# An attention block with its projections woven in: the fill between a slot's two logit products, and two engines in program order

## The chip, the cores and the metric

The kernel runs on one core of one Trainium2 chip. The metric is the device time of one execution in microseconds (us), lower is better; of several runs the median is taken. A profile shows one execution more closely.

The engines of the core run side by side, each through its own list of instructions, and meet by semaphores: TensorE (PE; its weight loads are listed as PEld), VectorE (DVE), ScalarE (ACT), GpSimd (POOL) and SyncE (SP), which here issues the transfers between HBM and the core's memory.

## The reference, cut to what matters

One transformer block over 2048 rows of 512, in float32: a layer norm modulated by a condition, "infini-attention" with 32 heads of 16 in four segments of 512 rows, a second modulated layer norm, and a bilinear feed-forward part of width 1376.

```python
mod = (silu(c) @ w_mod).reshape(1, 6, 1, -1)
sa, ca, ga, sb, cb, gb = mod[:, 0], ..., mod[:, 5]
h = layernorm(x) * (1 + ca) + sa
q, k, v = heads(h @ wq), heads(h @ wk), heads(h @ wv)       # 32 heads of 16, 4 segments of 512
phi = lambda t: where(t > 0, t + 1, exp(t))
for s in range(4):
    logits = q_s @ k_s.T * 0.25 + mask                      # within the segment, causal
    a_dot = softmax(logits) @ v_s
    a_mem = (phi(q_s) @ M) / (phi(q_s) @ z + 1e-6)
    out_s = g * a_mem + (1 - g) * a_dot                     # g = sigmoid(beta), per head
    M, z = M + phi(k_s).T @ v_s, z + phi(k_s).sum(rows)
x = x + ga * (out @ wo)
h = layernorm(x) * (1 + cb) + sb
return x + gb * (((h @ w_gate) * (h @ w_up)) @ w_down)
```

## The kernel before

**Order.** Every matmul and transposition goes through `pe`, which chains it to the one before: TensorE runs in the order in which the program text calls it, written out by hand. What VectorE, ScalarE, GpSimd and SP run is ordered by a scheduler, which plays the program through with its own costs and picks, on each engine, among the instructions that are ready. In the prologue alone (segment 0, group 0) VectorE and ScalarE are called through `CV` and `CA`, two objects of `class Chain`, which tie each instruction to the one before it on its engine, so that they too keep the program's order. `pin` ties single instructions to TensorE's place.

**The attention loop.** A unit is 4 heads of one segment, so there are 32 (`NQ`). The loop over `v` has five slots for each unit. A slot does one fifth of two different units:

- `q_step(u, i)`: logits with queries in rows, for the row maximum. The product goes to the PSUM bank `lq`, which exists once; two small matmuls add the mask, and VectorE reduces it (L261, tile `mxb`). The next `q` has to wait for that.
- `k_step(v, slot)`: logits again with keys in rows, with the negated maximum as two more rows of the operand. It goes to the bank `lk`, which exists once too; ScalarE takes the exponential (L295, tile `pt`), GpSimd sets the masked corner to zero (L298).
- `av_step` (slot 1): values times `pt` of the unit before, in bank `tb`, copied out by ScalarE as `tsb` (L324).
- `n_step` (slot 2): VectorE makes the negated maximum `nm` (L267), TensorE transposes it (`ntp`), VectorE writes it as two bfloat16 parts `nt` (L272, L273), and two transfers put it in rows 96 and 97 of `qst`, the operand of the next unit's `k`.
- `t_step` (slot 4): transposition of `tsb`, division by the sum (`rd`, `orow`, L345), and after every second unit a transfer to `od`.
- `fill(share[slot])`: the next pieces of what feeds later units and what follows done ones. Such a piece is mostly a block of three matmuls, ended by a `yield 0.68`. The shares are 0.25, 0, 0.25, 0.25, 0.25 of a rate. They run out of two generators: projections `kps`, `qps` (`a_kq`), values `vps` (`a_v`), layer norm (`ln`: `bn_stats` L139, normalisation L159, transposition `atp`/`ctp`, ScalarE's modulation L172), the memory part (`a_mem`: `mp`, `up`, `mz`), modulation rows (`mod`), and the output projection (`wo_op`: transposition `op` and copies `oH` L405, `oL` L408; `wo_mm`: `wops` and residual add L428).
- `load(v + 3)` at slot 1: transfers of `kst` and `qst` for a unit three further on.

**The end of a projection group.** When a group of `kps` or `qps` is complete, `a_kq` copies it out of PSUM as `f` (ScalarE, L632), splits it in three bfloat16 parts (high part on ScalarE L635, difference on GpSimd L636, middle part on ScalarE L637, rest on GpSimd L638), writes them out by three transfers to `kd` or `qd`, and, where the memory part needs phi, makes a relu and an exponential on ScalarE (L653, L654, called `rl` and `ph`) and joins them on VectorE (L658).

**The output weights.** `wo_prep` (woven in as `ob`) loads rows of `wo` (`wor`), scales them on GpSimd (L736), and splits them in `woH` (ScalarE, L748) and `woL` (GpSimd, L749), which `wops` needs.

After the loop stands the feed-forward part (`gps`, `ups`, `acc`).

Of the kernel before, what the change touches and what calls it, by code (L numbers as in the profile page):

```python
# [17 lines left out]
P = 128  # L18
# [27 lines left out]

@with_exitstack
def tile_kernel(ctx, tc, x, wq, wk_, wv, wo, beta, w_gate, w_up, w_down, c, w_mod, out):
# [31 lines left out]
    CV, CA = Chain(tc, nc.vector), Chain(tc, nc.scalar)  # L80
    cst = ctx.enter_context(tc.tile_pool(name="cst", bufs=1))
# [21 lines left out]
    nc.vector.memset(ones, 1.0)  # L103
    epst = cst.tile([P, 1], F32, name="epst")
    nc.vector.memset(epst, EPS)
    hmg = cst.tile([P, NG, HG, VS], F32, name="hmg")
    hm8 = cst.tile([P, HG], F32, name="hm8")
    nc.vector.tensor_reduce(hm8, ident.rearrange("p (d h) -> p h d", h=HG), axis=AX.X, op=ALU.add)
    for g in range(NG):
        nc.vector.tensor_copy(hmg[:, g], hm8.unsqueeze(2).to_broadcast([P, HG, VS]))  # L110
# [21 lines left out]
    def ln(pool, hpool, xt, s, sc, sh, pfx, hb, fast):  # L132

        first = pfx == "a" and s == 0
        V, A = (CV, CA) if first else (nc.vector, nc.scalar)
# [31 lines left out]
        for d in range(KT):  # L167
# [7 lines left out]
            if fast:  # L175
                V.tensor_copy(hi, h)
                V.tensor_sub(lo, h, hi.bitcast(F32))
            else:
                nc.scalar.activation(hi, h, AF.Copy)
                nc.gpsimd.tensor_sub(lo, h, hi.bitcast(F32))  # L180
# [30 lines left out]
    for a in mxb:  # L211
        nc.vector.memset(a, NEG)
    identb = ap.tile([P, P], BF, name="identb")
    nc.vector.tensor_copy(identb, ident)
    cmask = ap.tile([P, P], BF, name="cmask")
    nc.vector.memset(cmask, 0.0)
# [10 lines left out]
    def q_step(u, i):  # L227
# [33 lines left out]
        nc.vector.tensor_reduce(o, src, axis=AX.X, op=ALU.max)  # L261

    def n_step(u):
# [3 lines left out]
        nc.vector.tensor_reduce(nm, mxb[u % 2].rearrange("p h (q j) -> p (h q) j", j=4), axis=AX.X,  # L267
# [4 lines left out]
        nc.vector.tensor_copy(nt[:, 0], tp)  # L272
        nc.vector.tensor_sub(nt[:, 1], tp, nt[:, 0])  # L273
# [3 lines left out]
    def k_step(u, i):  # L277
# [17 lines left out]
        nc.scalar.activation(pt, kp, AF.Exp, scale=0.25)  # L295
# [6 lines left out]
    def av_step(u, kb):  # L302
# [19 lines left out]
        if kb == 2:  # L322
            tsbs[u] = ap.tile([P, L], F32, tag="tsb", name=f"tsb{u}", bufs=2)
            nc.scalar.activation(tsbs[u], tbs.pop(u), AF.Copy)  # L324

    def t_step(u):
# [15 lines left out]
        nc.vector.reciprocal(rd, tr[:, :, :, DH])  # L342
        og = omg[:, g * HG + h0:g * HG + h0 + 4]
        nc.vector.tensor_mul(rd, rd, og.unsqueeze(1).to_broadcast([P, 4, 4]))
        nc.vector.tensor_mul(orow[:, :, h0:h0 + 4, :], tr[:, :, :, 0:DH],  # L345
# [11 lines left out]
    def prep(i, pool, rpool, tag, nb):  # L357
# [9 lines left out]
        for nm in "gu":  # L367
# [3 lines left out]
            pin(nc.vector.tensor_copy(hi[:, :, 0:n], raw[:, :, 0:n]))  # L371
# [5 lines left out]
        pin(nc.vector.tensor_mul(rawd[0:n], rawd[0:n], gbb[0:n]))  # L377
        yield 0.0
        nc.scalar.activation(hi[0:n], rawd[0:n], AF.Copy)
# [14 lines left out]
    def wo_op(s, pb, rw, us, gs=range(NG)):  # L394

        for g in gs:
# [8 lines left out]
            nc.scalar.activation(oH, op, AF.Copy)  # L405
            us.append((oH, oL))
            yield 0.45
            pin(nc.vector.tensor_sub(oL, op, oH.bitcast(F32)))  # L408
# [18 lines left out]
    def wo_add(s, t, xr, ps):  # L427
        pin(nc.vector.tensor_add(xr, xr, ps))  # L428
        nc.sync.dma_start(x1d[s][t], xr)
# [42 lines left out]
    nc.vector.memset(wu, 0.0)  # L472
# [16 lines left out]
    nc.scalar.activation(e1, s_c, AF.Exp, scale=-1.0)  # L489
    nc.vector.tensor_scalar_add(e1, e1, 1.0)  # L490
    nc.vector.reciprocal(e1, e1)
    nc.vector.tensor_mul(s_c, s_c, e1)
    nc.scalar.activation(gg, be, AF.Exp, scale=-1.0)
    nc.scalar.activation(omg, be, AF.Exp)
    for tl in (gg, omg):
        nc.vector.tensor_scalar_add(tl, tl, 1.0)
        nc.vector.reciprocal(tl, tl)
# [4 lines left out]
    def mod_acc(r):  # L502
        for k in range(KT):
            pin(nc.scalar.activation(r[k], r[k], AF.Identity, scale=s_c[:, k:k + 1]))
# [4 lines left out]
    def cols(a, dst, nm):  # L509
# [3 lines left out]
        nc.vector.tensor_copy(dst, ps)  # L513

    def bcast(a, dst, nm):
        ps = bank(nm)
        MM(ps, ones, a, start=True, stop=True)
        nc.scalar.activation(dst, ps, AF.Copy)
# [48 lines left out]
    def load_g(nm, w, g):  # L567

        A, V = (CA, CV) if g == 0 else (nc.scalar, nc.gpsimd)
# [25 lines left out]
    def a_v(s):  # L595
        hH, hL = hcur[0]
        for t in range(4):
# [9 lines left out]
            nc.scalar.activation(vt[s % 2][t][:, 0:H * VS].rearrange("p (h e) -> p h e", e=VS)[:, :, 0:DH],  # L607
# [7 lines left out]
    def a_kq(s, g, nm):  # L615
# [3 lines left out]
        if True:  # L619
# [11 lines left out]
            A, V = (CA, CV) if fast else (nc.scalar, nc.gpsimd)  # L631
# [5 lines left out]
            (CV.tensor_copy if fast else nc.scalar.copy)(q3[:, 1, :], r)  # L637
            V.tensor_sub(q3[:, 2, :], r, q3[:, 1, :])  # L638
            for r0, n, k in ((0, 3, 0), (3, 2, 0), (5, 1, 0)) if nm == "k" else ((0, 1, 3), (3, 1, 2), (5, 1, 1)):
                if nm == "k":  # L640
                    nc.sync.dma_start(dst[s][g][r0:r0 + n].rearrange("r p t -> p r t"), q3[:, 0:n, :])
                else:
                    i = 3 - k
                    nc.sync.dma_start(dst[s][g][r0:r0 + k].rearrange("r p t -> p r t"),
                                      q3[:, i:i + 1, :].to_broadcast([P, k, L]))
            if (nm == "k" and s < NSEG - 1) or (nm == "q" and s > 0):
                if s == 0 and g == 0:
# [5 lines left out]
                nc.scalar.activation(rl, f, AF.Relu)  # L653
                nc.scalar.activation(e, f, AF.Exp)  # L654
# [23 lines left out]
    def a_mem(s, g):  # L678
# [3 lines left out]
        if s < NSEG - 1:  # L682
# [4 lines left out]
            nc.scalar.activation(pkr.rearrange("p a b -> p (a b)"), mp, AF.Copy)  # L687
            yield 0.5
        if s > 0:
# [3 lines left out]
            for i in range(2):  # L693
# [4 lines left out]
                nc.scalar.activation(ups[:, 2 * i:2 * i + 2], up, AF.Copy)  # L698
                yield 0.5
            pin(nc.vector.tensor_scalar_add(den, ups[:, :, :, DH], 1e-6))  # L700
            nc.vector.reciprocal(den, den)
            nc.gpsimd.tensor_mul(mem, ups[:, :, :, 0:DH], den.unsqueeze(3).to_broadcast([P, 4, HG, DH]))
            nc.sync.dma_start(memd[s][g], mem.rearrange("p t h e -> p (t h e)"))
        if s < NSEG - 1:
# [4 lines left out]
            if s == 0:  # L709
                nc.vector.tensor_mul(MZ[g], mz, hmg[:, g])  # L710
# [319 lines left out]
```

## Time and profile before

| | us |
|---|---|
| runs | 951.93, 954.98, 950.16 |
| median | 951.93 |
| profiled execution | 955.31 |
| its span (first to last instruction) | 953.6 |
| TensorE busy | 904.1 |
| VectorE, ScalarE, GpSimd busy | 461.8, 407.6, 315.6 |
| granted clock of TensorE, mean | 0.984 |

The profile's page gives the busy time of the engines, the chain of work that ended last, and the costliest groups, one in a line: line of the kernel, engine, operation, out<-in, shapes, count, then busy time and mean ns, then the idle time of the engine just ahead of these instructions and what released it. A timeline's row has start and duration in us, engine, line, operation, and in brackets the idle time ahead and its releaser. A row of the waits has the waiting operation, what it waited for, the total, the times and the longest. Rows of windows give start and end, length, busy time with the instruction count for PE, PEld, DVE, ACT and POOL, then the granted clock of TensorE (1.00 is full), the share of the DMA engines, and GB/s.

### The profile page before, as it was taken

What the parts mean: (1) busy time and instruction counts of PE and PEld (TensorE: products, weight loads), DVE (VectorE), ACT (ScalarE), POOL (GpSimd) and SP (SyncE); (2) the same over time, 40 slices, a digit from 0 to 9 for tenths busy, and PEclk for the clock granted to TensorE, in tenths of its full rate; (3) what the DMA queues carried; (4) which work ended last, traced back from release to release, by engine and by line L of the source; (5) the groups of instructions that cost most, each with busy time, mean ns of one, the idle gap of its engine ahead of it and who ended that gap; (6) DMA issues with size and microseconds to landing.
All of it is one profiled execution on the core that took longest, in us unless ns stands there. A gap on an engine that the chain in (4) does not pass through costs nothing.

```text
span 953.6 us, 14247 instructions
## 1 busy us (share of the span) xinstructions
PE 904.1 (95%) x5528; PEld 654.9 (69%) x5528; DVE 461.8 (48%) x756; ACT 407.6 (43%) x603; POOL 315.6 (33%) x457
## 2 busy tenths in 40 slices
PE   8979999999999999998998899999999999999998
PEld 5756657566566666665555577887888788878886
DVE  8566556675556755566457324544223223222112
ACT  3557757687575865577342621222111211221111
POOL 3255536465454753456522422562000000000000
PEclk9999999999999999999898899999999999999999
DMA  7574534654435544466661234432201020101011
GB/s 221 160 228 153 169 111 130 215 164 153 139 116 185 171 130 123 137 208 204 227 186 60 86 102 144 122 98 61 89 0 26 20 89 1 45 0 45 1 45 44
DMA packets 86211, 109.80 MB, mean 115 GB/s; under 512 B 9504, under 2 KB 58656, under 8 KB 86144
## 3 DMA queue, kind: packets, MB, share of 16 engines
q1 hardware_dynamic: 86000, 108.89, 36.8%
q8 instruction: 43, 0.70, 0.3%
q14 instruction: 24, 0.20, 0.1%
q10 hardware_dynamic: 144, 0.02, 0.0%
HBM read 67.98 MB, written 40.63 MB: 114 GB/s over the span
## 4 chain that ended last, share of the span: by engine, by line
PE 80%; DVE 7%; ACT 7%; DMA 3%; issue 1%; POOL 1%; SPq 0%; DVEq 0%; ACTq 0%; POOLq 0%
PE ups L966 13%; PE gps L966 13%; PE q L75 8%; PE tb L75 7%; PE k L75 6%; PE wops L75 5%; PE qps L75 4%; PE vps L75 3%; PE kps L75 3%; ACT pt L295 3%; DVE mxb L261 3%; PE acc2lq L987 2%; PE acc0lq L987 2%; PE acc3lq L987 2%; PE acc1lq L987 2%; PE acc1lk L987 2%
## 5 line engine op out<-in xcount | busy, mean ns | idle before, releaser
L261 DVE TENSOR_REDUCE mxb<-q 128x8 f32<-128x1024 f32 x160 | 195.5, 1222 | 161.2 <-PE q L75 160.8
L295 ACT ACTIVATE pt<-k 128x1024 f32<-128x1024 f32 x160 | 163.8, 1024 | 89.6 <-PE k L75 88.1
L298 POOL TENSOR_SCALAR_AFFINE_SELECT pt<-pt 128x256 f32<-128x256 f32 (+1 forms) x224 | 99.5, 458 | 202.5 <-ACT pt L295 194.5
L971 DVE TENSOR_TENSOR gs<-gs,ups 128x512 f32<-128x512 f32 (+1 forms) x44 | 30.2, 687 | 194.0 <-PE ups L966 194.0
L75 PE MATMUL q<-kst,qst 96*128 96x128 bf16 (+2 forms) x640 | 99.4, 278 | 14.8 <-DVE mxb L261 13.8
L75 PE MATMUL k<-qst,kst 98*128 98x384 bf16 (+3 forms) x512 | 98.1, 304 | 14.8 <-ACT pt L295 13.4
L970 ACT ACTIVATE gs<-gps 128x512 f32<-128x512 f32 (+1 forms) x44 | 26.2, 597 | 146.5 <-PE gps L966 146.5
L75 PEld LDWEIGHTS <-qst 96*128 96x128 bf16 x640 | 47.3, 99 | 54.4 <-issue 47.4
L974 ACT ACTIVATE mH<-gs 128x512 fp32r<-128x512 f32 (+1 forms) x44 | 27.8, 633 | 130.4 <-DVE gs L971 128.1
L75 PE MATMUL tb<-pt,v 128*32 128x512 f32 (+3 forms) x1024 | 76.6, 440 | 0.0
L966 PE MATMUL gps<-chH,gL 128*128 128x512 f32 (+1 forms) x176 | 69.3, 394 | 0.0
L966 PE MATMUL gps<-chH,gH 128*128 128x512 f32 (+1 forms) x176 | 69.3, 394 | 0.0
L966 PE MATMUL ups<-chH,uH 128*128 128x512 f32 (+1 forms) x176 | 69.3, 394 | 0.0
L966 PE MATMUL ups<-chL,uH 128*128 128x512 f32 (+1 forms) x176 | 69.3, 394 | 0.0
L966 PE MATMUL gps<-chL,gH 128*128 128x512 f32 (+1 forms) x176 | 69.3, 394 | 0.0
L966 PE MATMUL ups<-chH,uL 128*128 128x512 f32 (+1 forms) x176 | 69.2, 393 | 0.0
L75 PEld LDWEIGHTS <-kst 98*128 98x128 bf16 x512 | 41.5, 98 | 38.4 <-issue 31.7
L75 PEld LDWEIGHTS tb<-pt,v 128*32 128x32 f32 x1024 | 28.8, 110 | 46.2 <-issue 38.6
L75 PE MATMUL q<-cmask,identb 128*128 128x128 bf16 (+1 forms) x320 | 55.6, 255 | 0.0
L324 ACT ACTIVATE tsb<-tb 128x512 f32<-128x512 f32 x32 | 19.1, 597 | 75.0 <-PE tb L75 74.9
L153 POOL TENSOR_SCALAR cyb<-cmv 128x4 f32<-128x4 f32 x4 | 1.1, 276 | 142.8 <-DVE cmv L142 142.6
L975 DVE TENSOR_TENSOR mL<-gs,mH 128x512 fp32r<-128x512 f32 (+1 forms) x44 | 31.7, 720 | 28.7 <-ACT mH L974 28.5
(262 smaller groups left out, 1845.1 us busy)
## 6 DMA issues: line engine op xcount, KB each, us to landing
kst<-kd SPq DMA_DIRECT2D x32, 384.0 KB, 4.4
qst<-qd SPq DMA_DIRECT2D x32, 384.0 KB, 5.0
wm<-in_w_mod_dram SPq DMA_DIRECT2D x24, 256.0 KB, 5.4
kd<-k SPq DMA_DIRECT2D x16, 384.0 KB, 3.8
qd<-q SPq DMA_DIRECT2D x16, 384.0 KB, 3.2
x<-in_x_dram SPq DMA_DIRECT2D x16, 256.0 KB, 4.8
kd<-k SPq DMA_DIRECT2D x16, 256.0 KB, 3.7
qd<-q SPq DMA_DIRECT2D x16, 256.0 KB, 3.7
```

Source lines behind the costliest of these rows:

```text
L75: return pe(nc.tensor.matmul(*a, **k))
L153: eng.tensor_scalar(b, mv[:, :, 1], 1.0, EPS, op0=ALU.mult, op1=ALU.add)
L261: nc.vector.tensor_reduce(o, src, axis=AX.X, op=ALU.max)
L295: nc.scalar.activation(pt, kp, AF.Exp, scale=0.25)
L298: sels[u, i] = nc.gpsimd.affine_select(w, w, pattern=[[0, w.shape[1]], [1, P]], compare_op=ALU.is_ge, fill=0.0, base=0, channel_multiplier=-1)
L324: nc.scalar.activation(tsbs[u], tbs.pop(u), AF.Copy)
L966: nc.tensor.matmul(ps[0:n], a[:, k, 0:n], b[k], start=j == 0, stop=j == 11)
L970: nc.scalar.activation(gs[0:n], pss[0][0:n], AF.Copy)
L971: nc.vector.tensor_mul(gs[0:n], gs[0:n], pss[1][0:n])
L974: nc.scalar.activation(mH[0:n], gs[0:n], AF.Copy)
L975: nc.vector.tensor_sub(mL[0:n], gs[0:n], mH[0:n].bitcast(F32))
L987: nc.tensor.matmul(acc[t], a[0:n, t * P:(t + 1) * P], b[0:n, :], start=i == 0 and j == 0, stop=i == NF - 1 and j == 2)
```

## The change

1. In each slot the fill stands between `q_step` (with `av_step` or `t_step`) and `k_step`; before it stood behind `k_step`. `n_step` stays behind `k_step`, so it is behind the fill as well.
2. VectorE and ScalarE are called through `vec` and `act`, objects that pass each call on; during the attention loop they pass it to `CV` and `CA`. So both engines keep the order of the program there. GpSimd and SP do not.
3. In `a_kq` the middle part, GpSimd's last difference and the three transfers are now the function `rest()`, called after the next `yield 0.68`, one block later, except in the prologue.
4. Segment 1's layer norm, which is prepared during segment 0, was woven into the `Q` of group 2 and then `K` and `Q` of group 3; now it starts with the `K` of group 3, with four places there.
5. `ob` is woven into `wo_op(0)` alone, at four places; `wo_op(1)` comes as a whole after `wo_mm(0)` (before, its first two groups came ahead of it, with `ob` in between).

```diff
+class Switch:
+    def __init__(self, eng):
+        self.eng = eng
+    def __getattr__(self, name):
+        return getattr(self.eng, name)
...
+    vec, act = Switch(nc.vector), Switch(nc.scalar)
...
             A.activation(q3[:, 0, :], f, AF.Copy)
             V.tensor_sub(r, f, q3[:, 0, :])
-            (CV.tensor_copy if fast else nc.scalar.copy)(q3[:, 1, :], r)
-            V.tensor_sub(q3[:, 2, :], r, q3[:, 1, :])
-            for r0, n, k in ...: (three nc.sync.dma_start)
+            def rest():
+                (CV.tensor_copy if fast else act.copy)(q3[:, 1, :], r)
+                V.tensor_sub(q3[:, 2, :], r, q3[:, 1, :])
+                for r0, n, k in ...: (three nc.sync.dma_start)
+            if fast:
+                rest()
...
             yield 0.68
-            if nm in ph:
-                pin(nc.vector.scalar_tensor_tensor(e, e, 1.0, rl, op0=ALU.min, op1=ALU.add))
+            if not fast:
+                rest()
+            if phi:
+                pin(vec.scalar_tensor_tensor(e, e, 1.0, rl, op0=ALU.min, op1=ALU.add))
...
                     if g == 2:
                         xts[s + 1] = xload(s + 1)
                         lns = a_ln(s + 1)
-                        Q = weave(Q, lns, (0, 1, 2, 3))
+                        if s > 0:
+                            Q = weave(Q, lns, (0, 1, 2, 3))
                     else:
-                        K = weave(K, lns, (1,))
+                        K = weave(K, lns, (1,) if s > 0 else (0, 1, 2, 3))
                         Q = weave(Q, lns, (0, 1, 2, 3))
...
-        yield from weave(wo_op(0, pb, B["orl"], us[0]), ob, (1, 3))
-        yield from weave(wo_op(1, pb, o1, us[1], (0, 1)), ob, (0, 1))
+        yield from weave(wo_op(0, pb, B["orl"], us[0]), ob, (0, 1, 2, 3))
...
         yield from weave(wo_mm(0, us[0], pb), pr, (3, 6, 9, 12))
-        yield from wo_op(1, pb, o1, us[1], (2, 3))
+        yield from wo_op(1, pb, o1, us[1])
...
+    vec.eng, act.eng = CV, CA
     share = (0.25, 0.0, 0.25, 0.25, 0.25)
     for v in range(-2, NQ + 1):
...
             if prev and slot == 1:
                 for kb in (0, 1, 3, 2):
                     av_step(v - 1, kb)
-            if on:
-                k_step(v, slot)
-            if slot == 2 and 0 <= v + 1 < NQ:
-                n_step(v + 1)
...
             fill(share[slot], slot < 4)
+            if on:
+                k_step(v, slot)
+            if slot == 2 and 0 <= v + 1 < NQ:
+                n_step(v + 1)
...
     close(apool)
+    vec.eng, act.eng = nc.vector, nc.scalar
```

All other `nc.vector` and `nc.scalar` calls that the diff touches become `vec` and `act`, with nothing else changed. In the built programs TensorE's order of one unit (fill: `vps`, the number counts matmuls) is, one slot in a line:

```
before                        after
q_4 tb k_1                    q_4 tb k_1
q_0 k_2 ntp vps_0:6           q_0 vps_0:6 k_2 ntp
q_1 k_3 vps_0:6               q_1 vps_0:6 k_3
q_2 k_4 tr:4 vps_1:6          q_2 tr:4 vps_1:6 k_4
q_3 k_0 vps_1:6               q_3 vps_1:6 k_0
```

More of the change, by code (lines that the diff above doesn't have):

```diff
@@ L134, in ln @@
         first = pfx == "a" and s == 0
-        V, A = (CV, CA) if first else (nc.vector, nc.scalar)
+        V, A = (CV, CA) if first else (vec, act)
         mv = pool.tile([P, 4, 2], F32, tag="mv", name=f"{pfx}mv{s}", bufs=2)
@@ L211, in tile_kernel @@
     for a in mxb:
-        nc.vector.memset(a, NEG)
+        vec.memset(a, NEG)
     identb = ap.tile([P, P], BF, name="identb")
-    nc.vector.tensor_copy(identb, ident)
+    vec.tensor_copy(identb, ident)
     cmask = ap.tile([P, P], BF, name="cmask")
-    nc.vector.memset(cmask, 0.0)
+    vec.memset(cmask, 0.0)
     nc.gpsimd.affine_select(cmask, cmask, pattern=[[-1, P]], compare_op=ALU.is_ge,
@@ L636, in a_kq @@
             V.tensor_sub(r, f, q3[:, 0, :])
-            (CV.tensor_copy if fast else nc.scalar.copy)(q3[:, 1, :], r)
-            V.tensor_sub(q3[:, 2, :], r, q3[:, 1, :])
[L639 to L647, printed above, removed]
+            def rest():
+                (CV.tensor_copy if fast else act.copy)(q3[:, 1, :], r)
+                V.tensor_sub(q3[:, 2, :], r, q3[:, 1, :])
+                for r0, n, k in ((0, 3, 0), (3, 2, 0), (5, 1, 0)) if nm == "k" else ((0, 1, 3), (3, 1, 2), (5, 1, 1)):
+                    if nm == "k":
+                        nc.sync.dma_start(dst[s][g][r0:r0 + n].rearrange("r p t -> p r t"), q3[:, 0:n, :])
+                    else:
+                        i = 3 - k
+                        nc.sync.dma_start(dst[s][g][r0:r0 + k].rearrange("r p t -> p r t"),
+                                          q3[:, i:i + 1, :].to_broadcast([P, k, L]))
+            if fast:
+                rest()
+            phi = (nm == "k" and s < NSEG - 1) or (nm == "q" and s > 0)
+            if phi:
+                if fast:
                     yield 0.0
@@ L747, in open_b @@
         for k in range(KT):
-            pin(nc.scalar.activation(woH[:, k, :], raws[k], AF.Copy))
+            pin(act.activation(woH[:, k, :], raws[k], AF.Copy))
             nc.gpsimd.tensor_sub(woL[:, k, :], raws[k], woH[:, k, :].bitcast(F32))
```

99 lines of the change are left out of this document (50 added, 49 removed).

## The prediction

> **What bounds the kernel now.** I read the page first: the engines' shares, the chain that ended last, the costliest groups.
>
> ```profile
> span 953.6 us, 14247 instructions
> ...
> PE 904.1 (95%) x5528; PEld 654.9 (69%) x5528; DVE 461.8 (48%) x756; ACT 407.6 (43%) x603; POOL 315.6 (33%) x457
> ...
> PE 80%; DVE 7%; ACT 7%; DMA 3%; issue 1%; POOL 1%; SPq 0%; DVEq 0%; ACTq 0%; POOLq 0%
> ...
> L261 DVE TENSOR_REDUCE mxb<-q 128x8 f32<-128x1024 f32 x160 | 195.5, 1222 | 161.2 <-PE q L75 160.8
> L295 ACT ACTIVATE pt<-k 128x1024 f32<-128x1024 f32 x160 | 163.8, 1024 | 89.6 <-PE k L75 88.1
> ```
>
> TensorE is busy for 95% of the span and carries 80% of the chain. The change removes no matmul, so it can only win or lose in the 49.5 us in which TensorE idles, and in lost clock. Next the windows by stretch say where that idle time lies (start:end, length, busy time and count of each engine, granted clock, DMA share, GB/s):
>
> ```profile
> 50.00:100.00 50.00, 43.53 (x313) 28.81 (x311) 30.31 (x47) 33.07 (x50) 29.28 (x38) 0.93 0.62 197
> 100.00:200.00 100.00, 96.86 (x758) 63.49 (x761) 63.11 (x101) 67.11 (x97) 48.94 (x77) 1.00 0.50 152
> 200.00:300.00 100.00, 93.79 (x749) 62.54 (x742) 59.89 (x90) 68.07 (x99) 53.12 (x77) 1.00 0.47 145
> 300.00:400.00 100.00, 94.62 (x757) 62.50 (x756) 60.85 (x100) 62.24 (x92) 53.33 (x79) 1.00 0.48 148
> ...
> 450.00:500.00 50.00, 44.34 (x321) 28.10 (x320) 26.83 (x41) 20.93 (x26) 19.19 (x28) 0.93 0.66 212
> 500.00:550.00 50.00, 41.47 (x285) 27.07 (x284) 25.86 (x47) 22.63 (x32) 18.20 (x31) 0.86 0.22 74
> ...
> 600.00:953.00 353.00, 348.85 (x1533) 281.10 (x1531) 108.28 (x180) 65.36 (x108) 32.86 (x36) 1.00 0.14 45
> ```
>
> The feed-forward part (from 600 us) idles 4 us in 353; the change does not reach it. From 100 to 400 us 14.7 us are idle at full clock, spread thin. The stretches of 50 us at either end of the loop idle 6.5, 5.7 and 8.5 us, and the clock was granted only in part there: 0.07, 0.07 and 0.14 of 50 us, so about 3.5, 3.5 and 7 us more. Then TensorE's waits, asked for the attention loop, 50 to 550 us (total, times, longest):
>
> ```profile
> PE q L75 <- DVE mxb L261: 13.6, 16, 3.0
> PE k L75 <- ACT pt L295: 13.4, 21, 1.4
> PE op L78 <- DMA orl<-od: 3.8, 4, 3.1
> PE op L78 <- DVE oL L408: 2.0, 1, 2.0
> PE mz L75 <- DVE orow L345: 1.7, 1, 1.7
> ```
>
> Two single-buffered PSUM banks carry most of it: the next q waits until VectorE has reduced the last one (L261), the next k until ScalarE has taken its exponential (L295).
>
> **Part 1, fill between q and k.** This is the timeline where a unit's slot 1 has no fill: attention × values (tb), the copy of its result (tsb), k of slot 1, then q and k of slot 2.
>
> ```profile
> 478.64 0.60 ACT L324 ACTIVATE tsb<-tb 128x512 f32<-128x512 f32 x1 [3.36 <-PE tb L75]
> ...
> 479.21 1.02 ACT L295 ACTIVATE pt<-k 128x1024 f32<-128x1024 f32 x1
> ...
> 479.38 0.28 PE L75 MATMUL q<-cmask,identb 128*128 128x128 bf16 x2
> ...
> 480.28 0.60 PE L75 MATMUL k<-qst,kst 98*128 98x384 bf16 x4 [0.63 <-ACT pt L295]
> ...
> 481.07 0.40 PE L75 MATMUL wops<-woH,oL 128*128 128x512 f32 x1
> ...
> 481.31 0.40 PE L75 MATMUL wops<-woL,oH 128*128 128x512 f32 x1
> ```
>
> The exponential starts 0.6 us late because tsb stands before it, ends at 480.23, and k must wait 0.63. The fill (here wops) starts only behind k, though it waits for nothing. A fill matmul issues every 0.24 us (481.07, 481.31), so a block of three is 0.7 and the two blocks of a usual slot 1.4: between q and k they cover the wait whole. By the built order, 14 units have an empty slot 1 and 8 have one short transposition there. The 21 waits above hold 13.4 us, of which 4.1 lie in the last stretch (a row further on); 9.3 are left, and k starts 0.1 us later than the wait alone says in each of 17 (a release takes that long to be seen), 11 in all. Where slot 2's fill is a single block, or none, about 2 stay. Sum: **−9** (−8 to −12).
>
> **Part 2, VectorE in program order.** At two places VectorE, in the order that the scheduler chose, sat on an instruction that waited for a transfer, with a q reduction behind it:
>
> ```profile
> 66.07 0.69 DVE L139 BATCH_NORM_STATS2 ast<-x 128x6 f32<-128x512 f32 x1 [2.01 <-DMA x<-in_x_dram]
> ...
> 68.21 1.21 DVE L261 TENSOR_REDUCE mxb<-q 128x8 f32<-128x1024 f32 x1
> ...
> 69.47 1.01 PE L75 MATMUL q<-kst,qst 96*128 96x256 bf16 x4 [2.97 <-DVE mxb L261]
> ...
> 500.95 0.69 DVE L428 TENSOR_TENSOR xr<-xr,wops 128x512 f32<-128x512 f32 x1 [3.14 <-DMA qst<-nt]
> ...
> 502.83 1.01 PE L75 MATMUL q<-kst,qst 96*128 96x512 bf16 x2 [2.41 <-DVE mxb L261]
> ```
>
> In the changed order segment 1's LayerNorm statistics come with the K of group 3, well after x has landed, and the reduction stands before the residual add (L428). The stalls of 2.97 and 2.41 go, and with each the slow clock behind it: the windows that begin with them lost 3.5 us and half of 7. So **−6.4** and **−5.8**. (The row of the add names nt's transfer as its releaser; the add reads only xr and wops, so I take it as that of xr, on the same queue.) The cover: if x were late once more, or the add again ahead of a reduction, the whole of it comes back. After the first, LayerNorm's own work is next (in part 4); after the second nothing queues on the residual's transfer.
>
> The Trainium skill, "TensorE: Matmul & The Clock Gate", section "HAM oscillation — how this bites in real kernels", gives the rule that TensorE should have no idle gap over some 3.4 us. By that rule stalls of 2.97 and 2.41 us would cost no clock, and the two terms would be 6.8 us smaller together. The windows' clock of 0.93 and 0.86 says otherwise here, so the measurement is used.
>
> Of the remaining q waits (13.6 − 3.0 − 2.4 = 8.2 in 14) and the mz wait (1.7), some are of the same kind, with younger work ahead of a reduction; I take a fifth, **−2** (0 to −5). In the last stretch,
>
> ```profile
> PE k L75 <- ACT pt L295: 4.1, 4, 1.4
> ...
> PE op L78 <- ACT chf L172: 1.4, 1, 1.4
> ```
>
> exponentials stood behind the second LayerNorm's and wo's copies; in program order they come first in part: **−2** (−3 to +1).
>
> **Part 3, the wo hand-over.** All of wo's staging is now spread over wo_op(0), and wo_op(1) comes after wo_mm(0). The waits of op for orl (3.8) and oL (2.0) and a dip (3.5) go. What is late next is woL itself:
>
> ```profile
> 452.89 2.49 POOL L736 TENSOR_TENSOR wor<-wor,gab 128x512 f32<-128x512 f32 x2 [1.15 <-DMA wor<-in_wo_dram]
> ...
> 455.70 2.50 POOL L749 TENSOR_TENSOR woL<-wor,woH 128x512 fp32r<-128x512 f32 x2
> ```
>
> The last weights land before 452.89, and GpSimd needs two products and two differences at 1.25 each, until 458.2 at the best; wops now stands where op(1) stood, from about 449. Most of the 9.3 us comes back as this wait: **+0.5** (−5 to +5).
>
> **Part 4, ScalarE in program order.** This is the price. ScalarE's work behind a kq group, and an exponential that the order now puts behind it:
>
> ```profile
> 103.62 0.60 ACT L632 ACTIVATE kf<-kps 128x512 f32<-128x512 f32 x1 [0.42 <-PE kps L75]
> 104.25 0.63 ACT L635 ACTIVATE k<-kf 128x512 bf16<-128x512 f32 x1
> ...
> 105.31 0.61 ACT L654 ACTIVATE phk<-kf 128x512 f32<-128x512 f32 x1
> 105.83 1.00 ACT L295 ACTIVATE pt<-k 128x1024 f32<-128x1024 f32 x1
> 106.74 0.61 ACT L637 CAST k<-kr 128x512 bf16<-128x512 f32 x1
> ```
>
> ```profile
> L636 POOL TENSOR_TENSOR kr<-kf,k 128x512 f32<-128x512 f32 x15 | 17.9, 1196 | 7.0 <-ACT k L635 6.9
> ```
>
> From f to the exponential are 2.2 us. In before the exponential of a slot's k is ready while the fill still runs, so it goes ahead of the copies; now k stands behind the fill, and if the group ends in the fill's last block, four copies stand before its exponential. It then ends about 0.2 + 2.2 + 1.0 = 3.4 us after the fill. The next k comes after k, q and two blocks, 0.4 + 0.6 + 1.4 = 2.4 us: TensorE waits about 1.0, or 0.6 where a transposition stands between too. The built order has 11 such places (6 at 0.6, 5 at 1.0): 8.7. At 4 the group ends in the first block, and the third copy (L637) is ahead too, which waits for GpSimd's subtraction (1.2 us, the last row): 1.4 each, 5.5. LayerNorm's copies and normalisations ahead of an exponential or a reduction, and one place where both meet, give 5. Less the 4 us that before pays by now for the same cause outside slot 2: **+15** (+8 to +25).
>
> The late half of a group (rest(): third copy, GpSimd's difference, three transfers on SP) goes out one block later. That is 0.7 us, more where GpSimd takes the next fill's work first, for rows of kd and qd that the load of a later unit fetches. On SP the three transfers fall behind whatever the block between issued, and loads queue behind them. No wait of TensorE above is on a kst or qst load, so I take 0; with that cover gone it is 0.7 for each of the 15 pairs of groups, 10.
>
> **Part 5, the nm step.** In before nm's reduction stood ahead of slot 2's q reduction, and ntp on TensorE behind k. Now nm is behind that q's reduction and behind the fill's VectorE work. The reduction ends about 1.4 us after q, the two blocks and k take 1.8: covered. With one block or none ntp waits 0.3 to 1.0, and TensorE's order is fixed, so the next q waits with it. Some ten units: **+4** (0 to +12).
>
> **The sum.** Gains 9 + 6.4 + 5.8 + 2 + 2 = 25.2, costs 0.5 + 15 + 4 = 19.5, so −5.7 on the profiled execution, whose time is 955.31 us (1.7 around its span): 949.6. It lies 3.4 above the median of 951.93, about one dip of the clock; on the median the forecast is **946.2**, faster.
>
> **Rivals.** *The ScalarE queue decides (slower).* If the exponential waits the full 1.05 us in all 24 groups that have four copies (part 4), that is 25 rather than 15, and with nm at 8, the small gains at −1 and part 1 at −8: 25 + 8 + 0.5 − 8 − 6.4 − 5.8 − 1 = +12.3, 964. For it: of the 89.6 us that ScalarE idled before L295, 88.1 went by waiting for k, so most exponentials now start at once and have a place to lose. Against: only 15 places have the group's end where it hurts. It decides from part 4 + part 5 over 25 us.
>
> *New dips (no change).* Stalls of 2.4 and 3.0 us cost 3.5 us of clock each. Stacked waits (ScalarE's copies and GpSimd's subtraction) come near 2.5 at one place, woL's wait at another. Two dips give −5.7 + 7 = +1.3, 953.
>
> *The copies are covered (much faster).* If other work between two k (transpositions, tb) hides most of part 4, it is 8, part 5 is 1: 9.5 − 25.2 = −15.7, 936.
>
> That the change would not do what it says is excluded for its order: the built program has fill between q and k in each slot, and both engines chained.
>
> **How the numbers follow.** A measurement of this kernel can tell about 0.5%, 4.8 us (the three runs lie 4.8 apart). Forecast 0.38, of which 0.28 lies beyond 4.8 us and 0.10 within; the covered case 0.18; dips 0.14, of which 0.10 within and 0.04 slower; the queue 0.30. So faster 0.46, same 0.20, slower 0.34. The range takes in the covered case and the queue with a little of their own spread: 932 to 966. The forecast's own range is 941 to 951.
>
> **What would show it.** In the changed profile the waits of k for pt in slot 2, and the dips near 69 and 502 us, are gone (clock 1.00 in 50 to 100); there are waits of k for pt of about 1 us behind the ends of kps and qps, some of ntp's followers for nm, and one of wops for woL near 450 us. Part 4 is wrong if k's waits for pt total under 5 or over 20 us. The forecast as a whole is wrong if the windows of 100 to 400 us, as they now are, hold clearly more idle time than before.

## The result: slower by 1%

The changed kernel takes 962.5 us (median of 6 runs, 959.03 to 964.35) against 952.5 for the kernel before (6 runs beside it, 950.16 to 954.98): a ratio of 1.0099, 95% interval 1.0073 to 1.0125. The forecast was 946.2. The result lies outside the forecast's own range, inside the whole range, and on the other side of no change. In time, the rival in which ScalarE's queue decides (964) is the nearest; its sum is set against the runs further down.

From the page of the changed kernel (instructions that go through a chain all show the line of the helper, L39):

```profile
span 962.0 us, 14246 instructions
...
PE 910.0 (95%) x5527; PEld 656.7 (68%) x5528; DVE 466.0 (48%) x756; ACT 413.2 (43%) x603; POOL 313.8 (33%) x457
...
PE 76%; ACT 6%; DVE 5%; issue 4%; DMA 4%; POOL 3%; SPq 1%; DVEq 0%; POOLq 0%; ACTq 0%
```

The engines' work is the same. TensorE has 52 us without work instead of 49.5, and its chain share fell by 4 points. Its waits in the loop (waits of TensorE, 50 to 556 us):

```profile
PE k L85 <- ACT pt L39: 19.5, 22, 2.0
PE ntp L88 <- DVE nm L39: 6.2, 11, 1.1
PE wops L85 <- POOL woL L768: 3.2, 2, 1.7
PE q L85 <- DVE mxb L39: 3.2, 5, 1.3
PE atp L88 <- DVE x L39: 2.4, 3, 1.1
PE mz L85 <- DVE den L39: 2.1, 1, 2.1
```

The q waits fell from 13.6 to 3.2, the waits of op for orl are gone. The waits of k for pt rose from 13.4 to 19.5, and those of ntp for nm (none before) and of wops for woL are new: the three that the prediction named. To see where the time went, the first tb of a unit serves as a milestone; here are the stretches between such milestones in the traces, in us (the last column ends with the start of the last matmul):

```
                        to first  q to    2nd to    25th tb to    feed-
                        q         2nd tb  25th tb   feed-forward  forward
before                  41.2      52.9    344.1     138.5         371.7
changed                 43.1      57.1    358.1     127.0         371.6
```

The last part of the loop won 11.5, the middle lost 14, the first segment lost 4.2 where 6.4 were to be won. The 1.9 ahead of the first q is in no edit's reach: that stretch took 40.4 to 44.0 in the traces of all runs below, whatever the kernel. It goes with the clock granted there: 40.4 and 40.5 where none was lost, 43.1 to 44.0 where 6.8 us of it were.

Why the middle loses, in the timeline where a group of qps ended and the fill (kps) goes on:

```profile
419.85 0.60 ACT L39 ACTIVATE qf<-qps 128x512 f32<-128x512 f32 x1 [0.66 <-PE qps L85]
...
420.85 1.29 POOL L361 TENSOR_TENSOR orow<-orow,memb 128x512 f32<-128x512 f32 x1 [0.82 <-DVE orow L39]
...
422.09 1.16 POOL L647 TENSOR_TENSOR qr<-qf,q 128x512 f32<-128x512 f32 x1
...
422.55 0.39 PE L85 MATMUL kps<-ahL,wkH 128*128 128x512 f32 x1
...
423.29 0.62 ACT L39 CAST q<-qr 128x512 bf16<-128x512 f32 x1 [1.13 <-POOL qr L647]
...
423.81 1.02 ACT L39 ACTIVATE pt<-k 128x1024 f32<-128x1024 f32 x1
...
424.88 0.90 PE L85 MATMUL k<-qst,kst 98*128 98x512 bf16 x2 [1.94 <-ACT pt L39]
```

GpSimd is busy with orow until 422.1 and only then makes the difference qr. ScalarE stands idle for 1.13 us at the third copy, which needs qr; the exponential of a k that TensorE issued at 420.35 stands behind it and starts at 423.81, and the next k waits 1.94. The granted clock then falls: 0.93 in the stretch from 425 to 450,

```profile
425.00:450.00 25.00, 24.13 (x187) 15.08 (x186) 13.12 (x20) 15.19 (x22) 10.53 (x18) 0.93 0.51 159
```

where before had 1.00. One sign that the prediction named is missing: the clock in 50 to 100 us is 0.90, not 1.00. The one that it named for being wrong is there: the windows from 100 to 400 us hold 18.3 us without work, where before held 14.7.

```profile
50.00:100.00 50.00, 41.74 (x267) 27.48 (x264) 29.83 (x44) 29.25 (x43) 26.55 (x35) 0.90 0.58 175
100.00:200.00 100.00, 95.43 (x743) 61.51 (x741) 62.42 (x94) 65.75 (x95) 47.91 (x75) 1.00 0.49 150
200.00:300.00 100.00, 92.83 (x717) 61.59 (x717) 60.16 (x92) 68.21 (x98) 53.86 (x76) 0.98 0.47 142
300.00:400.00 100.00, 93.47 (x747) 60.52 (x746) 61.31 (x97) 63.43 (x90) 48.82 (x75) 1.00 0.47 144
```

In the first segment, the layer norm's four normalisations and nm stand in the same queue of VectorE:

```profile
87.89 0.54 DVE L39 TENSOR_SCALAR x<-x,amv,ay 128x512 f32<-128x512 f32 x1
...
88.35 0.21 DVE L39 TENSOR_REDUCE nm<-mxb 128x16 f32<-128x64 f32 x1
...
88.61 0.28 PE L88 MATMUL ntp<-ident,nm 128*16 128x128 f32 x1 [0.69 <-DVE nm L39]
...
89.48 1.22 DVE L39 TENSOR_REDUCE mxb<-q 128x8 f32<-128x1024 f32 x1
...
90.62 2.39 DVE L39 TENSOR_SCALAR x<-x,amv,ay 128x512 f32<-128x512 f32 x3
...
91.21 0.79 PE L88 MATMUL atp<-ident,x 128*128 128x128 f32 x2 [0.91 <-DVE x L39]
...
93.06 0.33 PE L88 MATMUL atp<-ident,x 128*128 128x128 f32 x1 [1.06 <-DVE x L39]
```

A q reduction of 1.22 us goes ahead of the normalisations that atp waits for, since the program names it first.

### The profile page after: what moved, and what is told of

It is laid out like the page before. It is cut to its first block, busy times and chain, and to the rows that moved or that the text cites. A ratio compares the mean times of both kernels' runs of the same rounds, so it can differ in the third digit from the quotient of the medians.

```text
span 962.0 us, 14246 instructions
## 1 busy us (share of the span) xinstructions
PE 910.0 (95%) x5527; PEld 656.7 (68%) x5528; DVE 466.0 (48%) x756; ACT 413.2 (43%) x603; POOL 313.8 (33%) x457
## 4 chain that ended last, share of the span: by engine, by line
PE 76%; ACT 6%; DVE 5%; issue 4%; DMA 4%; POOL 3%; SPq 1%; DVEq 0%; POOLq 0%; ACTq 0%
PE gps L987 13%; PE ups L987 13%; PE q L85 8%; PE tb L85 7%; PE k L85 6%; PE wops L85 4%; PE vps L85 3%; PE kps L85 3%; DVE mxb L39 2%; ACT pt L39 2%; PE qps L85 2%; PE acc2lq L1008 2%; PE acc0lq L1008 2%; PE acc3lq L1008 2%; PE acc1lq L1008 2%
## 5 line engine op out<-in xcount | busy, mean ns | idle before, releaser
L39 DVE TENSOR_REDUCE mxb<-q 128x8 f32<-128x1024 f32 x160 | 195.6, 1222 | 153.6 <-PE q L85 153.3
L39 ACT ACTIVATE pt<-k 128x1024 f32<-128x1024 f32 x160 | 163.3, 1021 | 81.4 <-PE k L85 80.4
L85 PE MATMUL k<-qst,kst 98*128 98x384 bf16 (+3 forms) x512 | 98.5, 305 | 20.0 <-ACT pt L39 19.5
L85 PEld LDWEIGHTS <-qst 96*128 96x128 bf16 x640 | 53.7, 99 | 28.9 <-issue 8.2
L85 PEld LDWEIGHTS tb<-pt,v 128*32 128x32 f32 x1024 | 28.7, 110 | 45.8 <-issue 40.5
L39 ACT ACTIVATE tsb<-tb 128x512 f32<-128x512 f32 x32 | 19.1, 597 | 54.3 <-PE tb L85 54.3
```

What stands on the lines that cost most here:

```text
L39: i = getattr(self.eng, name)(*a, **k)
L85: return pe(nc.tensor.matmul(*a, **k))
```

## The experiments

Ratios are against the kernel before, run beside each, with their 95% intervals.

### Program order, taken away as a whole and by half

```diff
-    vec.eng, act.eng = CV, CA          # run 1: no chain in the loop
+    vec.eng = CV                       # run 3: VectorE chained, ScalarE free
```

> The changed kernel with VectorE and ScalarE left to the scheduler in the loop again; the slot order, rest() and the other edits stay. If program order on the two engines is the loss (the prediction's parts 4 and 5), k waits for pt and ntp for nm mostly go and the time falls to 945-952. If the new slot order itself is the loss, whatever the order on the engines, it stays at 958-965.

> The changed kernel with VectorE in program order and ScalarE left to the scheduler. If the exponential behind the group's copies is the main price (part 4), k's waits for pt fall from 19.5 us to under 10 and the time to 948-954. If nm behind the fill on VectorE (part 5) or the first segment is the price, it moves by less than 4, 958-964.

Without chains 937.95 (0.9855, 0.9828 to 0.9882), well under both kernels and under what was expected; with VectorE alone chained 949.3 (0.998, 0.9962 to 0.9999). So program order costs 24.5 us by the medians, 23 by the ratios. With ScalarE freed 13 come back (11 by the ratios), with VectorE freed too another 11 (12); VectorE was not freed alone. Without chains TensorE's waits for the exponential are a third, and ntp waits for nm nowhere:

```profile
PE k L85 <- ACT pt L306: 6.8, 11, 1.2
```

All else in the change together is worth 13. The rest of the question is what lies in the 24.5 and in the 13.

### The old slot order under the chains

```diff
+            if on:                     # k_step and n_step directly behind av_step again,
+                k_step(v, slot)        # ahead of the fill; chains and all else as changed
+            if slot == 2 and 0 <= v + 1 < NQ:
+                n_step(v + 1)
...
             fill(share[slot], slot < 4)
-            if on:
-                k_step(v, slot)
...
```

> The changed kernel with k_step and n_step ahead of the fill again, everything else changed (both engines in program order). If the chains lose by themselves (VectorE and ScalarE blocked behind waiting instructions), it stays above 958. If they lose only together with the new slot order (exponential and nm behind the fill's copies), it comes to 945-953: part 1's gain of 9 is lost, but parts 4 and 5 go, and part 2's gains stay.

981.67 (1.0314, 1.0284 to 1.0343): the chains lose by themselves, and more in the old order, 40 us above the same edits without chains (941.53, below). The new slot order makes program order cheaper, not dearer; the second reading of the expectation is wrong. TensorE's waits in that run:

```profile
PE ntp L88 <- DVE nm L39: 18.1, 30, 1.4
PE k L85 <- ACT pt L39: 13.9, 22, 1.5
PE q L85 <- DVE mxb L39: 13.6, 18, 1.7
```

With no fill between, only k stands between q and ntp, and ntp waits for nm, behind q's reduction, in 30 of 32 units: part 5's wait without its cover.

### The slot order and the other edits, each alone and without chains

> The kernel before with only the fill moved between q_step and k_step; no program order on VectorE and ScalarE, no other edit. If the slot order is what makes the first of these runs (everything but the chains, ratio 0.986) fast, this gives nearly all of it: 936-942, k's waits for pt down from 13.4 to about 6. If the other edits (late rest(), layer norm, wo) carry it, it stays at 946-952.

> The changed kernel without the chains and with the old slot order: late rest(), layer norm and wo's order alone. If the slot order carries the gain, 946-952; if these edits do, 937-943. Beside the second run (chains with the old slot order, 981.7) it gives the chains' price in the old order: over 28 if the two are independent of nothing, about 24 if the price is the same in both slot orders.

```diff
+            fill(share[slot], slot < 4)        # slot order alone, in the kernel before
             if on:
                 k_step(v, slot)
...
-    vec.eng, act.eng = CV, CA          # other edits alone: no chain, and k_step ahead of the fill
```

The first is the kernel before with the two calls moved; the second has only late rest(), the layer norm and the wo edit. 941.47 (0.9878, 0.9851 to 0.9906) and 941.53 (0.9877, 0.9856 to 0.9898): each is worth 11, both together 13 or 14, so the two gains do not add up. The stretches:

```
                        q to    2nd to    25th tb to
                        2nd tb  25th tb   feed-forward
before                  52.9    344.1     138.5
slot order alone        52.5    341.5     128.9
other edits alone       46.9    343.6     132.6
both, no chains         51.9    342.9     126.2
changed (with chains)   57.1    358.1     127.0
```

Both mend the last part, 9.6 and 5.9 alone and 12.3 together, so some of it is the same time there. In the first segment 0.4 and 6.0 became 1.0, and part of that is the one execution that was traced, 3.2 above its run's median: a k waits 1.90 for nt's transfer at 62.90, and half clock from 64.1 to 70.9 us takes 3.4 more. Where the rest of the shortfall lies, single traces do not show. In the middle, where part 1 of the prediction had its 14 units, the slot order wins just 2.6. The timeline of slot 2 in it shows that the wait itself is gone:

```profile
114.18 0.40 PE L75 MATMUL vps<-wvH,ahL 128*128 128x512 f32 x1
114.42 0.40 PE L75 MATMUL vps<-wvL,ahH 128*128 128x512 f32 x1
114.65 0.61 PE L75 MATMUL k<-qst,kst 98*128 98x384 bf16 x4
115.10 0.27 PE L78 MATMUL ntp<-ident,nm 128*16 128x128 f32 x1
115.22 0.60 PE L75 MATMUL q<-kst,qst 96*128 96x256 bf16 x4
```

Slot by slot against before (differences over 0.25 us counted), 22 slots of the middle are shorter, most of them slot 2 by 0.65, in sum 11.7 us. But 10 are longer by 8.4, and 6.7 of that is in five with a memory piece in the fill, such as

```profile
181.16 1.17 PE L75 MATMUL mz<-v,pkr 128*128 128x136 f32 x8 [2.10 <-DVE orow L345]
```

There k stands behind a piece that itself waits, or behind copies.

### nm early, and ScalarE's copies out of the chain

```diff
+            if slot == 2 and 0 <= v + 1 < NQ:      # nm early
+                nm_step(v + 1)                     # nm's reduction alone
             if 0 <= u < NQ:
                 q_step(u, i)
...
-            A, V = (CA, CV) if fast else (act, nc.gpsimd)          # copies free: f, high part,
+            A, V = (CA, CV) if fast else (nc.scalar, nc.gpsimd)    # third copy, rl, ph unchained
...
-                (CV.tensor_copy if fast else act.copy)(q3[:, 1, :], r)
+                (CV.tensor_copy if fast else nc.scalar.copy)(q3[:, 1, :], r)   # third copy free: this alone
```

> The changed kernel with nm's reduction put ahead of slot 2's q_step in the program, so ahead of its reduction on VectorE; the transposition stays behind k. If part 5 of the prediction names the cost, ntp's waits for nm (6.2 us in 11) go and the time falls by 4-7, to 956-959. If nm's lateness is covered by k's other waits, under 2 of it comes back.

> The changed kernel with ScalarE's six instructions behind a kps or qps group left out of the chain, all others in program order. If the exponential behind these copies, and behind the third copy that waits for GpSimd, is ScalarE's share of the loss (part 4), it comes to within 3 of the run with ScalarE free: 948-953, k's waits for pt under 10 us. If another of ScalarE's instructions blocks (tsb, layer norm's, the output projection's copies), it stays above 957.

> The changed kernel with both: nm's reduction ahead of slot 2's q, and the group's ScalarE copies out of the chain; all else in program order. If parts 4 and 5 are two separate costs, their two measured gains (7.3 and 9.4) add up: 944-948. If each only uncovers the other (ntp's wait and the exponential's in the same slots), less than 12 comes in all: 950 or more.

> The changed kernel with only the third copy of a group (the one that waits for GpSimd's difference) left out of ScalarE's chain; the four copies ahead stay in it. If an exponential behind a copy that itself waits (as at 423 us: the copy idles 1.1 us, k then 1.9) is the main part of ScalarE's loss, 5-9 us come back: 954-958. If the four copies' own 2.2 us are, under 3 comes back: 960 or more.

> The changed kernel with nm's reduction early and the third copy out of the chain. If the two costs are separate, their single gains (7.3 and 7.6) add up: 945-949. If they hide behind each other as in the run with all copies free, 951-954.

nm early gives 955.22 (1.0023, 1.0006 to 1.0041), 7.3 less, and ntp's waits are gone from the trace. All copies of a group free (five instructions; the expectation says six): 953.14 (1.0012, 0.9995 to 1.0029), 9.4 less. The third copy alone: 954.9 (1.0037, 1.0017 to 1.0057), 7.6 less. By the ratios these are 8.3 and 5.9, each about 2 either way: most of the gain comes with the one copy that waits, but what the four that work cost is not settled. k's waits for pt, 19.5 in the changed kernel, first with the third copy free, then with all, fall by 5.0 for the one and by another 5.3 for the four:

```profile
PE k L85 <- ACT pt L39: 14.5, 21, 2.0
```

```profile
PE k L85 <- ACT pt L39: 9.2, 11, 2.0
```

But nm early with all copies free gives 951.57 (1.0003, 0.9987 to 1.0019), and with the third copy free 953.4 (1.0012, 0.9997 to 1.0027): the two do not add up, 9 to 11 in all (8 to 9 by the ratios). A TensorE that waits less at one place reaches the next queue sooner: with nm early alone, k's waits for pt are 21.3 instead of 19.5. That this is the whole reason is not shown. Some 14 us of the chains' price stay when the two named causes are gone; the trace of the last run has k's waits for pt still at 15.3, wops for woL 3.8, atp for x 2.4. They are spread, and were not taken apart further.

### rest() at once

```diff
-            if fast:
-                rest()
+            rest()
...
-            if not fast:
-                rest()
```

> The changed kernel with rest() called at once, as before, not a block later; chains and all else stay. The third copy then stands directly behind the second and waits for GpSimd's 1.2 us, with relu, exponential and the next pt behind it, in all 30 groups. If blocked waits in program order are the mechanism, this is clearly slower than the changed kernel: 972-990. If ScalarE's queue has room for it, it stays at 959-966.

1024.67 (1.0784, 1.0745 to 1.0823), 62 slower than the changed kernel and beyond what was expected. First waits of TensorE, then of ScalarE (50 to 620 us):

```profile
PE k L85 <- ACT pt L39: 59.5, 30, 3.1
```

```profile
ACT q L39 <- POOL qr L647: 25.5, 15, 3.1
ACT k L39 <- POOL kr L647: 20.7, 14, 3.5
```

In the changed kernel the latter two are 5.9 and 6.9. The third copy now blocks ScalarE for 1.6 us in each of 29 groups, and k waits in 30 places for 2.0 each. The block's delay of rest() is thus worth 62 us, but only under the chain, as the next run shows.

### The other edits one by one, on the kernel before

```diff
+                        if s > 0:                      # layer norm alone, in the kernel before
+                            Q = weave(Q, lns, (0, 1, 2, 3))
...
-        yield from weave(wo_op(0, pb, B["orl"], us[0]), ob, (1, 3))          # wo alone
-        yield from weave(wo_op(1, pb, o1, us[1], (0, 1)), ob, (0, 1))
+        yield from weave(wo_op(0, pb, B["orl"], us[0]), ob, (0, 1, 2, 3))
...
+            if not fast:                               # rest() alone, behind the yield
+                rest()
```

> The kernel before with segment 1's layer norm moved as in the change, and nothing else. If that edit, and not program order on VectorE, takes away the stall of 2.97 us at 69 us and its dip (the prediction's part 2, first place), 945-948. If the scheduler finds another transfer to wait for there, 950-954.

> The kernel before with only the wo edit (all of the weights' staging in wo_op(0), wo_op(1) behind wo_mm(0)). The first run without chains and with the old slot order gained 11, of which the layer norm gives about 5. If the wo edit gives the rest, 944-948, with the op waits for orl near 450 us gone. If late rest() does, it stays at 950-954.

> The kernel before with rest() called a block later and nothing else changed. If the late half of a group is what is left of the other edits' gain (11 less 4 and 4), 947-949. If it does nothing where the scheduler orders ScalarE anyway, 950.5-953.5.

The layer norm's move alone: 947.9 (0.9963, 0.9945 to 0.9981); the wo edit alone: 947.9 (0.9957, 0.9934 to 0.9979); late rest() alone: 953.07 (1.0013, 0.9993 to 1.0033), nothing that can be told from no change. The first takes the first segment from 52.9 to 47.0 us with no clock lost, as part 2 said, with no chain. (In the wo run it takes 48.8 and in the run with late rest() 49.1, with x's statistics still ahead of the reduction: x came 0.6 to 0.8 us earlier, q waits 2.26 and 2.24 instead of 2.97, and no dip follows. So some 4 of the 6.4 were the luck of one execution.) The wo edit takes the last part from 138.5 to 132.5 (with the layer norm's move alone it takes 136.0, with late rest() alone 134.9). The sum of the three is 7 or 8 where all together gave 11; the remaining 3 or 4 are not explained, and each of the four figures is uncertain by about 2.

```diff
-                        if s > 0:                      # in the changed kernel: woven as before
-                            Q = weave(Q, lns, (0, 1, 2, 3))
+                        Q = weave(Q, lns, (0, 1, 2, 3))
...
+                        K = weave(K, lns, (1,))
```

> The changed kernel with segment 1's layer norm woven as in the kernel before (from Q of group 2). If moving it is what costs TensorE time between 50 and 100 us (atp waiting for x, all normalisation at once), 3-5 us faster than the changed kernel, 957-960. If x's transfer then holds VectorE in program order ahead of a q reduction, as the scheduler's order did at 66 us, it is 1-5 us slower, 963-968.

Under the chains the layer norm's place does not matter: 961.24 (1.0101, 1.007 to 1.0132), as the changed kernel and between the two ranges that were expected. Woven early, it puts nm behind statistics that wait for x's transfer, and ntp waits 1.81 at 69.92; woven late, its normalisations stand in each other's way, as shown above.

### k where it wins

```diff
+            early = v < 25 and not (slot == 2 and v in SPLIT)   # where it wins
+            if early:
+                kn()                                             # k_step, n_step ahead of the fill
...
+            fill(share[slot], slot < 4, kn if v < 25 and not early else None)   # k behind the first block
+            if v >= 25:
+                kn()                                             # k behind the whole fill
```

> The changed kernel without chains, and with k placed behind the first block of a slot's fill, not behind the whole: q, block, k, block. One block (0.7 us) covers slot 2's wait of 0.65, and an exponential is no longer behind a group that ends in the last block. If that is what took back the slot order's gain between 94 and 438 us, 931-936. If a block between two k is too little, because a k comes sooner behind the one before, 938-945.

> The same with the old order (k ahead of the fill) in all slots but slot 2, where k stands behind the first block. If slot 2's wait is all that the slot order has to win, and the other slots only lose by it, 931-935, at or below the run before. If slot 3 then waits for slot 2's exponential (two k closer together), 937-941, no better than the fill wholly between (937.95).

> No chains, all other edits, and k behind fill only where the traces of the runs show a win: in slot 2 of the 12 units whose fill there is projection blocks (k behind the first block), and in all slots of the last units (from v = 25). Summed from the slots: 47 to the second tb, 337 on to the 25th, 126 to the feed-forward part: 926-931. If the wins of slot 2 are given back in later slots (the time sits in VectorE's and ScalarE's queues, not in the slot), 935-940.

All three have no chains and all other edits. k behind the first block everywhere: 943.85 (0.992, 0.9899 to 0.9941); only in slot 2: 943.67 (0.9925, 0.9907 to 0.9943). The first lies in the second range of its expectation, the second above both of its ranges: neither brings the gain that was hoped for. In the first, the largest loss of one slot (3.1 us) has the memory piece mz ahead of k. In the second, against the other edits alone, slot 2 wins 0.3 to 0.7 wherever the block ahead of k is not a memory piece; it loses 0.4 to 1.4 in seven units, all of them with a memory piece there. So SPLIT holds the 12 units in which that trace shows a win, most of them with projection blocks alone, and from unit 25 on k is behind the whole fill: 932.76 (0.98, 0.9767 to 0.9834), the fastest of all, 2% under before. Its stretches are 46.5, 337.6 and 125.5, where 47, 337 and 126 were summed; the median is 2 above the expected range; the profiled execution spent 44.0 to the first q. Two windows of it, to set against before's:

```profile
50.00:100.00 50.00, 46.70 (x352) 31.66 (x351) 34.16 (x53) 34.97 (x52) 33.72 (x44) 1.00 0.69 211
100.00:200.00 100.00, 98.93 (x782) 64.69 (x781) 65.21 (x106) 70.47 (x104) 49.71 (x79) 1.00 0.50 154
```

## Why the prediction was wrong

- **Part 1 (−9).** The mechanism and its gross size were right: 0.65 a slot, 11.7 in the middle with the slot order alone. The net there is 2.6, mostly because k behind a memory piece waits with it. Part 4 counted costs of k behind the fill only where the chains make them; this one is there without them. That the slot order alone measured 11 in all, near the 9, is luck: 9.6 of it lie in the last part, which the 9 mostly left out. (The 0.1 added for each wait fits, 0.65 won for waits of 0.57 to 0.62. The reason given for it does not: in all 21 of these waits k starts 0.05 after the exponential's end.)
- **Part 2 (−6.4, −5.8, −2, −2), the step that failed first.** This part put 16.2 of gains under VectorE's program order (the first by way of the layer norm's move). Measured, program order on VectorE costs 11: 949.3 with it chained, 937.95 without. The gains came, but smaller, and from the layer norm's move, the wo edit and the slot order, with no chain. With the chains, the first stall is gone, and others stand in its place: 57.1 us in that segment, where 47 were possible with the old slot order and no chain. TensorE's waits of the changed kernel from 50 to 100 us:

```profile
PE q L85 <- DVE mxb L39: 2.3, 2, 1.3
PE k L85 <- ACT pt L39: 2.1, 2, 1.3
PE atp L88 <- DVE x L39: 2.0, 2, 1.1
PE ntp L88 <- DVE nm L39: 1.0, 2, 0.7
```

  The second stall (2.41 at 502 us) did stay away, and the unit around it is 5.0 shorter. But 3.3 to 3.8 of that are the luck of before's one execution as well. With the layer norm's move alone, late rest() alone and the slot order alone, the same add still stands ahead of a reduction and waits for xr's own transfer, 1.94 to 2.35 us instead of 3.14; q waits 1.21 to 1.61, no half clock follows there, and the unit is 17.0 to 17.5 long instead of 20.8. With late rest() alone:

```profile
497.87 0.69 DVE L428 TENSOR_TENSOR xr<-xr,wops 128x512 f32<-128x512 f32 x1 [1.94 <-DMA xr<-in_x_dram]
```

```profile
499.75 0.59 PE L75 MATMUL q<-kst,qst 96*128 96x512 bf16 x2 [1.21 <-DVE mxb L261]
```

  A stall and its dip read from one execution were booked in full, twice.
- **Part 3 (+0.5).** Wrong sign of the small sum: the wo edit alone wins 4. woL's wait is there (3.2), as named, and is smaller than what goes.
- **Part 4 (+15).** k's waits for pt, 19.5 us, are within the 5 to 20 that were allowed. Freeing ScalarE gave 13, near the 15. But the copy that waits for GpSimd is worth 6 to 8 of it (5.0 of these waits). It was counted at 4 places of 30, with GpSimd free, for 5.5; at 423 us GpSimd was behind with orow. The four copies of 2.2 us make another 5.3 of the waits.
- **Part 5 (+4).** nm put early is worth 7.3, waits of 6.2 in 11 places: right place, near the estimate, inside its range.
- **The sum.** Parts 4 and 5 were to cost 19 and program order measured 24.5. That is not far off, and against it stand 13 of gains. The prediction credited 16.2 to part 2 on top of part 1's 9, as if separate; slot order and other edits win 11 each but 13 or 14 together. So the 25.2 of gains were about half that, the costs 5 more, and −5.7 became +10. The rival's 964 is near by luck: it had 25 for ScalarE's queue, which measured 13, and left part 1 nearly whole at −8 and part 2's two stalls whole.
- The prediction's remark that idle gaps under 3.4 us cost clock here held: the 1.94 us at 424.88 is followed by the window with 0.93. By the rule in the Trainium skill's "HAM oscillation — how this bites in real kernels" ("TensorE: Matmul & The Clock Gate") it would cost none.

## What to carry to other kernels

An engine kept in program order is blocked by the first instruction that waits for a slower engine: look for copies that need another engine's result, and count where that engine is itself late, before fixing an order. Gains of several edits need not add up; run them together, and compare stretch by stretch to see which may be the same time. A stall and a dip that one trace shows can be that execution's own: look for the same place in a second trace before counting on it. Work put between two steps hides a wait only if that work does not itself wait: place it by what the piece is, not by slot.

## What was not expected of the hardware

The granted clock falls after waits shorter than those of part 2: in the loop half clock lasted 3.4 or 6.8 us at a time, in the changed kernel after single waits of 1.94 and 2.08 us. In each trace the dips in the loop start on one raster of 3.41 us, and what goes with a dip is TensorE's idle time summed over one stretch of that raster. Over all 20 traces (30 to 570 us), the 75 stretches just ahead of a dip held 1.29 to 3.15 us without work, and no other stretch at full clock held more than 1.93. The wait of 2.26 in the wo run, at 70.82, fell in two stretches, 0.7 and 1.6, and cost no clock. This is a reading of traces; no run tests it. The time to the first q varied from 40.4 to 44.0 us between executions of code that no run changed, with the clock lost there; so a difference under 3 us in one trace's total says little, and the stretches were compared instead.
